# Six instead of seven chunks of the first MLP beside attention, and the fetch of a narrow input as a step of its own

## The chip, the cores and the metric

One core of one Trainium2 chip runs the kernel. The metric is the device time of one execution in microseconds; the figure for the kernel before is a median of 3 runs. Engines: PE is TensorE (PEld its weight loads), DVE VectorE, ACT ScalarE, POOL GpSimd, SP the engine whose queue issues the DMAs here.

## The reference

Attention over 4 batches, 8 heads, 576 positions and 64 dimensions, mixed with a read from a memory matrix, and then two MLPs in a row over the 2304 = 4 x 576 tokens, all in float32 accuracy:

```python
def _attn_ref(q, k, v, M_prev, z_prev, beta):        # q, k, v: (4, 8, 576, 64)
    scores = scale * np.matmul(q, k.transpose(0, 1, 3, 2))   # causal
    ...                                              # softmax, a @ v -> local
    mem_out = einsum(phi(q), M_prev) / (einsum(phi(q), z_prev) + 1e-06)
    g = 1.0 / (1.0 + np.exp(-beta))
    return g * mem_out + (1 - g) * local
x = attn_out.transpose(0, 2, 1, 3).reshape(2304, 512)
h = x @ w_in                                         # (512, 2048)
x = where(h > 0, h, exp(min(h, 0)) - 1) @ w_out      # first MLP
h = x @ w_in2
out = maximum(0.01 * h, h) @ w_out2                  # second MLP
```

The MLP weights come in as 64-bit floats, so the kernel fetches pairs of 32-bit words and decodes them.

## The kernel before

Products are made float32-accurate by splitting an operand into a high and a low part (xh, xl; gh, gl; two layers of w), three matmuls for one. The 2048 hidden units of an MLP are 16 chunks of 128. A chunk's weights (`load_w`, L92) are fetched raw, 1 MB in two DMAs, and decoded by ACT, DVE and POOL into the two layers; beside attention in halves through a PSUM bank, later whole, through one staging tile `wm` (one buffer from then on).

Attention runs batch by batch, 4 head pairs a batch. Each output of the product with v (`pv`, L498) goes to DRAM: for batch 0 into `xm`, for the others, where a head's rows carry two halves that still have to be added, into `xq`.

The first MLP is done in two ways. Its first `NFA` chunks are done **narrowly**, beside attention: each batch is cut into 2 parts of 288 tokens, 8 parts in all. `phase1_units` (L658) makes the list of steps of a batch's two parts. For each part: `u_x` fetches the input into the tile x (and, for batches 1 to 3, the other halves into y), adds the halves on DVE, splits the sum on ACT and POOL and writes the split parts to DRAM for later; then one `u_h` for each chunk, 12 matmuls of 288 columns into a `pm` bank, the activation (`elu`, ACT twice, DVE) and its split (ACT or DVE, POOL); then 4 `u_o`, 3 `NFA` matmuls each, whose result goes to DRAM. x and y have one buffer, xh and xl one for each of the two parts, gh and gl `NG` buffers, as many as there are chunks.

The other chunks are done **widely** after attention, in four tiles of 512 tokens and one of 256, with gh and gl in 3 buffers; narrow and wide results are added. The second MLP uses tiles of the same size and all 16 chunks.

What sets the order: the list of attention's steps has nominal costs of PE time. When the last step of a batch is listed, the steps of its narrow parts are appended to a list `fill`, due `DELAY` = 13000 ns of nominal cost later; from then on each attention step earns credit (`rate`, L749), and a fill step is put in when its cost is earned. `RESERVE` = 60000 ns of nominal cost is left for after attention, where `merge` (L706) mixes the remaining steps with the fetch and decode of the first `NPRE` = 6 of the wide chunks; the others follow in the first wide tile. The weights of the second MLP go into the slots of the narrow chunks during the later wide tiles and into those of the wide chunks after them. The order in this list is not the order on the engines. A planner at build time walks the whole program with estimated times and puts on each engine what is ready by then, earlier in the list first; a block under `high_priority(offset=FILL_OFF)` counts as 20 places earlier. What it lays down is fixed: on the chip an engine that comes to an instruction whose input has not landed stands there. The weights of the narrow chunks are in `wpa` and have a slot each; those of the wide chunks, in `wpb`, lie where attention's tiles were, so their fetch begins when attention has ended.

## Time and profile before

| | us |
|---|---|
| median of 3 runs | 1100.0 (1098.87 to 1101.18) |
| the profiled execution | 1098.26 |
| its span | 1096.2 |
| PE busy in the span | 1057.6 (96%) |
| DVE, ACT, POOL busy | 600.3, 484.8, 530.6 |
| granted TensorE clock, mean | 0.995 |

An engine's busy time is the sum of its instructions without overlap; PE's matmuls are pipelined, so the distance from one start to the next tells a matmul's cost better than its duration. A line such as L644 is a line of the kernel. "Idle before" in square brackets is the time an engine stood still ahead of an instruction, with what it was put down to. In the chain of waits each piece is a stretch of the work that ended last.

### The profile page before, as it was taken

What the parts mean: (1) busy time and instruction counts of PE and PEld (TensorE: products, weight loads), DVE (VectorE), ACT (ScalarE), POOL (GpSimd) and SP (SyncE); (2) the same over time, 40 slices, a digit from 0 to 9 for tenths busy, and PEclk for the clock granted to TensorE, in tenths of its full rate; (3) what the DMA queues carried; (4) which work ended last, traced back from release to release, by engine and by line L of the source; (5) the groups of instructions that cost most, each with busy time, mean ns of one, the idle gap of its engine ahead of it and who ended that gap; (6) DMA issues with size and microseconds to landing.
All of it is one profiled execution on the core that took longest, in us unless ns stands there. A gap on an engine that the chain in (4) does not pass through costs nothing.

```text
span 1096.2 us, 17406 instructions
## 1 busy us (share of the span) xinstructions
PE 1057.6 (96%) x5904; PEld 912.7 (83%) x5904; DVE 600.3 (55%) x1398; ACT 484.8 (44%) x1169; POOL 530.6 (48%) x674
## 2 busy tenths in 40 slices
PE   6998899989998999999999999999999999999997
PEld 3777789979998999978877889888888888888896
DVE  6889987778878857566574314664321222232232
ACT  5988877777877645444343223432211110111110
POOL 7675675667667626455453224755422322222221
PEclk9999999999999999999999999999999999999999
DMA  7753643564365139665653304331200100010010
GB/s 181 189 144 91 188 115 99 124 169 145 78 178 156 59 81 271 225 215 185 219 189 119 98 18 116 135 116 39 77 1 1 58 20 1 1 39 1 1 39 20
DMA packets 151576, 115.05 MB, mean 105 GB/s; under 512 B 81728, under 2 KB 144192, under 8 KB 151488
## 3 DMA queue, kind: packets, MB, share of 16 engines
q1 hardware_dynamic: 151488, 113.95, 35.5%
q8 instruction: 47, 0.77, 0.3%
q14 instruction: 41, 0.34, 0.1%
HBM read 78.52 MB, written 31.85 MB: 101 GB/s over the span
## 4 chain that ended last, share of the span: by engine, by line
PE 73%; DMA 8%; DVE 7%; POOL 3%; ACT 3%; SPq 3%; issue 3%; DVEq 0%; POOLq 0%; ACTq 0%
PE pm L616 17%; PE sc L876 14%; PE tp L616 13%; PE sc L644 8%; PE po L876 4%; PE pm L644 4%; PE po L522 3%; PE tp L455 3%; PE po L644 2%; DMA wraw<-in_moe_w_out_dram 2%; DMA x<-xq 2%; SPq L212 2%; PE sc L426 1%; PE sc L427 1%; PE pm L522 1%
## 5 line engine op out<-in xcount | busy, mean ns | idle before, releaser
L623 POOL TENSOR_TENSOR gl<-e,gh 128x512 fp32r<-128x512 f32 (+2 forms) x181 | 199.8, 1108 | 369.8 <-DVE gh L241 291.9
L616 PE MATMUL tp<-xw,w 128*128 128x512 f32 (+1 forms) x504 | 145.4, 371 | 0.9 <-DVE e L630 0.9
L616 PE MATMUL pm<-xw,w 128*128 128x512 f32 (+1 forms) x496 | 143.9, 371 | 0.0
L876 PE MATMUL sc<-w,gh 128*128 128x512 f32 x448 | 137.7, 393 | 0.0
L449 POOL TENSOR_SCALAR pt<-pt,rs,omg 128x128 f32<-128x128 f32 (+4 forms) x160 | 102.7, 651 | 28.0 <-DVE rs L444 25.7
L616 PEld LDWEIGHTS tp<-xw,w 128*128 128x128 f32 x504 | 91.3, 188 | 19.7 <-DVE e L630 1.7
L644 PE MATMUL sc<-gh,w 128*128 128x512 f32 (+2 forms) x438 | 106.0, 343 | 1.1 <-DVE st L857 0.7
L616 PEld LDWEIGHTS pm<-xw,w 128*128 128x128 f32 x496 | 90.5, 188 | 18.5
L434 ACT ACTIVATE pt<-pt,mx 128x128 f32<-128x128 f32 (+4 forms) x160 | 93.2, 585 | 22.7 <-DVE mx L429 22.1
L876 PEld LDWEIGHTS sc<-w,gh 128*128 128x128 f32 x448 | 83.1, 188 | 17.9
L616 PE MATMUL tp<-xv,w 128*128 128x512 f32 (+1 forms) x252 | 93.2, 370 | 0.0
L616 PE MATMUL pm<-xv,w 128*128 128x512 f32 (+1 forms) x248 | 92.0, 371 | 0.0
L616 PE MATMUL pm<-xh,w 128*128 128x288 f32 x368 | 80.2, 305 | 9.1 <-DVE e L630 5.7
L635 ACT ACTIVATE e<-pm 128x512 f32<-128x512 f32 (+1 forms) x40 | 22.2, 556 | 150.3 <-PE pm L616 149.1
L455 PE MATMUL tp<-ident,pt 128*128 128x128 f32 x480 | 80.1, 276 | 8.0 <-DVE al L248 3.1
L241 DVE CAST gh<-e 128x512 fp32r<-128x512 f32 (+2 forms) x146 | 77.9, 537 | 16.9 <-PE po L644 4.2
L137 POOL TENSOR_TENSOR w<-wm,w 128x512 fp32r<-128x512 f32 x50 | 66.1, 1344 | 43.4 <-ACT w L239 43.4
L876 PE MATMUL sc<-w,gl 128*128 128x512 f32 x224 | 85.4, 393 | 0.0
L644 PEld LDWEIGHTS sc<-gh,w 128*128 128x128 f32 x438 | 74.6, 188 | 12.2 <-issue 1.5
L636 DVE TENSOR_TENSOR e<-tp,e 128x512 f32<-128x512 f32 (+1 forms) x40 | 25.5, 637 | 107.2 <-ACT e L635 107.1
L636 DVE TENSOR_TENSOR e<-pm,e 128x512 f32<-128x512 f32 (+1 forms) x40 | 25.5, 637 | 105.8 <-ACT e L635 105.8
L429 DVE CUSTOM_DVE_ANT_0 pt<-sc,mask 128x128 f32<-128x128 f32 (+4 forms) x160 | 69.4, 446 | 8.6 <-PE sc L427 4.3
(155 smaller groups left out, 2407.9 us busy)
## 6 DMA issues: line engine op xcount, KB each, us to landing
wraw<-in_moe_w_in_dram SPq DMA_DIRECT2D x32, 512.0 KB, 4.1
wraw<-in_moe_w_out_dram SPq DMA_DIRECT2D x32, 512.0 KB, 5.3
xh<-xh SPq DMA_DIRECT2D x8, 576.0 KB, 3.3
xl<-xl SPq DMA_DIRECT2D x8, 576.0 KB, 3.9
ys<-st SPq DMA_DIRECT2D x32, 144.0 KB, 3.0
x1s<-st SPq DMA_DIRECT2D x36, 128.0 KB, 1.9
x<-x1s SPq DMA_DIRECT2D x9, 512.0 KB, 3.9
out_dram<-st SPq DMA_DIRECT2D x36, 128.0 KB, 1.7
```

The lines of the kernel that those rows point to most:

```text
L137: nc.gpsimd.tensor_tensor(out=w[:, 1, a], in0=t[:, a], in1=_f(w)[:, 0, a], op=ALU.subtract)
L241: (nc.vector if eng == "V" else nc.gpsimd).tensor_copy(dst, src)
L429: nc.vector.tensor_tensor_reduce(out=pt[0:m, k0:k0 + n], in0=sc[0:m, 0:n], in1=mk, op0=ALU.add, op1=ALU.min, scale=-0.125, scalar=mx[0:m, ...
L434: nc.scalar.activation(out=pt[0:m, 0:nk], in_=pt[0:m, 0:nk], func=AF.Exp, scale=-1.0, bias=mx[0:m, last:last + 1], accum_out=self.pd["ss"] ...
L449: nc.gpsimd.tensor_scalar(out=pt, in0=pt, scalar1=rs[0:m, i:i + 1], scalar2=omg[0:m, h:h + 1], op0=ALU.mult, op1=ALU.mult,)
L455: nc.tensor.transpose(dst, self.p[c][:, k0:k0 + kn], ident)
L522: nc.tensor.matmul(po[:, a:b], w, x, start=i == 0, stop=i == len(mms) - 1)
L616: nc.tensor.matmul(ph, wi[:, wj, kc, :], xx[:, kc, :], start=n_mm == 0, stop=n_mm == 11)
L623: nc.gpsimd.tensor_tensor(out=gl, in0=g, in1=_f(gh), op=ALU.subtract)
L636: nc.vector.tensor_tensor(out=t, in0=ph, in1=t, op=ALU.max)
L644: nc.tensor.matmul(py, wo[:, wj, ec * P:(ec + 1) * P], gg, start=opens and f == first and n_mm == 0, stop=closes and f == last and n_mm == 2,)
L876: nc.tensor.matmul(pos[tb], gg[:, tb * P:(tb + 1) * P], wo[:, wj, :], start=f == 0 and n_mm == 0, stop=f == NF - 1 and n_mm == 2,)
```

## The change

`NFA` and `NG` go from 7 to 6. `u_x` is cut into `u_load`, which issues the DMAs of a part's input, and `u_x`, which adds, splits and stores. Part 0's `u_load` is called as soon as its batch's last attention step is listed, ahead of the delay and outside the high priority; part 1's stands after the second `u_h` of part 0, and its `u_x` after the fifth `u_h` of part 0, ahead of the sixth and of the four `u_o`.

```diff
--- before.py
+++ after.py
@@ -44,7 +44,7 @@
     DFF = w1i.shape[1] // 2
     NKC = DM // P
     NF = DFF // P
-    NFA = 7
+    NFA = 6
     NPRE = 6
     NR = 3
     EB = 3
@@ -60,7 +60,7 @@
     TN = 256
     TW = 512
     NTT = NT // TN
-    NG = 7
+    NG = 6
     DSPAN = 0.75
     RESERVE = 60000.0
     EARLY = 150
@@ -657,32 +657,31 @@
 
     def phase1_units(ti):
 
-        units = []
-        for pi, (pt, o, w, _) in enumerate(parts):
-            if pt != ti:
-                continue
-            st = {}
-
-            def u_x(pi=pi, o=o, w=w, st=st):
-                def split():
-                    st["x"] = split_x(xt, w, pi % 2)
-                    for n in range(2):
-                        nc.sync.dma_start(xp_scr[n][pi], _f(st["x"][n]))
-                    st["g"] = {}
-
-                xt = mtile("x", 1, F32, (NKC, NW))[:, :, 0:w]
-                if ti < V32:
-                    nc.sync.dma_start(xt, xm_scr[ti][:, :, o:o + w])
-                    split()
-                    return
-                x2 = mtile("y", 1, F32, (NKC, NW))[:, :, 0:w]
-                for j in range(2):
-                    ps, pz = slice(64 * j, 64 * j + 64), slice(64 - 64 * j, 128 - 64 * j)
-                    nc.sync.dma_start(xt[ps], xq_scr[ti][j][ps, :, o:o + w])
-                    nc.sync.dma_start(x2[ps], xq_scr[ti][j][pz, :, o:o + w])
+        mine = [(pi, o, w, {}) for pi, (pt, o, w, _) in enumerate(parts) if pt == ti]
+
+        def u_load(pi, o, w, st):
+            xt = st["t"] = mtile("x", 1, F32, (NKC, NW))[:, :, 0:w]
+            if ti < V32:
+                nc.sync.dma_start(xt, xm_scr[ti][:, :, o:o + w])
+                return
+            x2 = st["t2"] = mtile("y", 1, F32, (NKC, NW))[:, :, 0:w]
+            for j in range(2):
+                ps, pz = slice(64 * j, 64 * j + 64), slice(64 - 64 * j, 128 - 64 * j)
+                nc.sync.dma_start(xt[ps], xq_scr[ti][j][ps, :, o:o + w])
+                nc.sync.dma_start(x2[ps], xq_scr[ti][j][pz, :, o:o + w])
+
+        def u_x(pi, o, w, st):
+            xt = st["t"]
+            if ti >= V32:
                 for c in range(NKC):
-                    nc.vector.tensor_tensor(out=xt[:, c], in0=xt[:, c], in1=x2[:, c], op=ALU.add)
-                split()
+                    nc.vector.tensor_tensor(out=xt[:, c], in0=xt[:, c], in1=st["t2"][:, c], op=ALU.add)
+            st["x"] = split_x(xt, w, pi % 2)
+            for n in range(2):
+                nc.sync.dma_start(xp_scr[n][pi], _f(st["x"][n]))
+            st["g"] = {}
+
+        units = [(0, lambda: u_x(*mine[0]))]
+        for k, (pi, o, w, st) in enumerate(mine):
 
             def u_h(f, w=w, st=st):
                 ph = h_bank()[:, 0:w]
@@ -696,12 +695,15 @@
                 copy(E_Y, y, py)
                 nc.sync.dma_start(y_scr[pi][:, ec], y)
 
-            units.append((0, u_x))
             for f in range(NFA):
                 units.append((HC * 12 * w / 2.4, lambda f=f, u=u_h: u(f)))
+                if k + 1 < len(mine) and f == 1:
+                    units.append((0, lambda k=k: u_load(*mine[k + 1])))
+                if k + 1 < len(mine) and f == NFA - 2:
+                    units.append((0, lambda k=k: u_x(*mine[k + 1])))
             for ec in range(NKC):
                 units.append((3 * NFA * w / 2.4, lambda ec=ec, u=u_o: u(ec)))
-        return units
+        return lambda: u_load(*mine[0]), units
 
     def merge(a, bu):
         ta = sum(c for c, _ in a) + 1.0
@@ -759,7 +761,9 @@
         if done == 0:
             close_decode()
         if done is not None:
-            fill += [(pos + DELAY, c2, u2) for c2, u2 in phase1_units(done)]
+            fetch, more = phase1_units(done)
+            fetch()
+            fill += [(pos + DELAY, c2, u2) for c2, u2 in more]
         if fill and fill[0][0] <= pos:
             credit += c * rate
         while fill and fill[0][0] <= pos and fill[0][1] <= credit:
```

## Rows read from the trace of the kernel before

**Rows 1.** Stages: us, busy (count) of PE, PEld, DVE, ACT, POOL, clock, DMA, GB/s.

```profile
0.00:104.00 104.00, 91.82 (x472) 69.52 (x473) 84.42 (x249) 84.94 (x234) 69.11 (x133) 1.00 0.59 153
104.00:211.00 107.00, 100.05 (x750) 94.97 (x750) 90.81 (x267) 83.46 (x241) 72.63 (x118) 1.00 0.47 128
211.00:313.00 102.00, 96.58 (x727) 94.07 (x726) 81.58 (x250) 77.85 (x221) 68.57 (x110) 0.98 0.53 137
313.00:404.00 91.00, 85.98 (x646) 83.65 (x645) 69.26 (x199) 61.31 (x171) 53.31 (x81) 0.98 0.40 112
```

**Rows 2.** Slices of 10 us beside attention, same columns.

```profile
130.00:140.00 10.00, 9.20 (x67) 8.43 (x66) 9.88 (x24) 8.52 (x27) 8.51 (x12) 1.00 0.76 220
...
240.00:250.00 10.00, 7.41 (x44) 7.08 (x45) 7.93 (x24) 7.38 (x22) 8.02 (x12) 0.83 0.63 178
```

**Rows 3.** Order of time on PE: stalls ahead of a narrow input's first matmuls.

```profile
121.37 0.81 PE L616 MATMUL pm<-xh,w 128*128 128x288 f32 x4 [1.85 <-ACT xh L239]
...
222.27 0.53 PE L616 MATMUL pm<-xh,w 128*128 128x288 f32 x2 [1.52 <-ACT xh L239]
...
244.50 0.53 PE L616 MATMUL pm<-xh,w 128*128 128x288 f32 x2 [2.59 <-DVE e L630]
...
338.16 0.85 PE L616 MATMUL pm<-xh,w 128*128 128x288 f32 x2 [2.83 <-DVE e L630]
```

**Rows 4.** Chain of waits: start us, us, a narrow and a wide run.

```profile
395.63 3.20 PE tp L616 x24
...
526.75 2.80 PE tp L616 x12
```

**Rows 5.** Order of time on PE: starts of two hidden chunks, last wide tile.

```profile
669.01 0.40 PE L616 MATMUL pm<-xw,w 128*128 128x256 f32 x2
...
670.41 0.40 PE L616 MATMUL tp<-xw,w 128*128 128x256 f32 x2
```

**Rows 6.** Order of time on SP: first weight fetch after attention.

```profile
408.18 0.53 SPq L102 DMA_DIRECT2D wraw<-in_moe_w_in_dram  x1
```

**Rows 7.** Order of time on POOL: ends of the wide chunks' decodes, nine in all.

```profile
422.94 2.62 POOL L137 TENSOR_TENSOR w<-wm,w 128x512 fp32r<-128x512 f32 x2
...
465.69 2.54 POOL L137 TENSOR_TENSOR w<-wm,w 128x512 fp32r<-128x512 f32 x2 [5.57 <-ACT w L239]
473.80 2.95 POOL L137 TENSOR_TENSOR w<-wm,w 128x512 fp32r<-128x512 f32 x2 [5.57 <-ACT w L239]
...
503.27 2.54 POOL L137 TENSOR_TENSOR w<-wm,w 128x512 fp32r<-128x512 f32 x2 [4.23 <-ACT w L239]
```

**Rows 8.** L644 (narrow outputs) by stage: us, busy (count) of PE, PEld, clock, DMA, GB/s.

```profile
104.00:211.00 107.00, 23.38 (x139) 19.69 (x140) 1.00 0.47 128
211.00:313.00 102.00, 27.30 (x164) 22.83 (x163) 0.98 0.53 137
313.00:404.00 91.00, 22.59 (x130) 18.62 (x130) 0.98 0.40 112
```

**Rows 9.** L616 (narrow hidden units) in the third of these stages, same columns.

```profile
313.00:404.00 91.00, 28.53 (x168) 24.68 (x168) 0.98 0.40 112
```

**Rows 10.** Order of time on POOL: decodes beside the second MLP's start, first and last.

```profile
681.20 2.60 POOL L137 TENSOR_TENSOR w<-wm,w 128x512 fp32r<-128x512 f32 x2
...
759.57 2.54 POOL L137 TENSOR_TENSOR w<-wm,w 128x512 fp32r<-128x512 f32 x2
```

**Rows 11.** Chain of waits: the second MLP's sixteenth chunk in its first tile.

```profile
768.60 2.80 PE tp L616 x12
```

**Rows 12.** Order of time on SP: batch 1's loads and the store before them.

```profile
192.79 0.54 SPq L681 DMA_DIRECT2D x<-xq  x1
...
211.03 0.41 SPq L530 DMA_DIRECT2D xq<-xp  x1
...
214.12 0.54 SPq L681 DMA_DIRECT2D x<-xq  x1
```

**Rows 13.** Order of time on DVE: the add on the same input.

```profile
221.29 2.17 DVE L684 TENSOR_TENSOR x<-x,y 128x288 f32<-128x288 f32 x4 [4.79 <-issue]
```

## The prediction

> **What bounds the kernel now.** I read the page's busy shares first, then the busy time by stage, then tens of microseconds inside the attention stage, then the order of time on SP, PE, DVE and POOL where PE falls short. TensorE is busy nearly everywhere: in the three stages in which attention and the first MLP's narrow parts run together, 104 to 404 us, it has 100.05, 96.58 and 85.98 us of 300, so it idles 17.4 us there [rows 1]. The reader is to see that DVE is never far behind (90.81 of the first 107 us), and that in a slice such as 130 to 140 it is DVE at 9.88 of 10 that sets the pace and PE that has room [rows 1, 2]. The kernel is therefore bound by PE's total work, plus some 17 us of stalls beside attention, plus what the weight decode lets through when attention ends.
>
> The stalls beside attention lie where a narrow part's input arrives. PE stood 1.85, 1.52, 2.59 and 2.83 us before the first matmuls on a new input (part 0 of batch 0, part 0 and part 1 of batch 1, part 1 of batch 2), 8.8 us in all [rows 3]. The one at 244.5 has a second cost: the granted clock of these ten microseconds is 0.83, a mean over 2.4 GHz and its half, so 1.7 us more are lost [rows 2].
>
> **Part 1: chunks moved from narrow to wide.** A chunk costs, in the narrow form, 24 matmuls in each of 8 parts, 192 of 288 columns. A run of 24 lasts 3.20 us, so one starts every 0.133 us, and the chunk is 192 x 0.133 = 25.6 us [rows 4]. In the wide form it is 24 matmuls in each of four tiles of 512 columns and one of 256. Twelve of the first take 2.80 us (0.233 each) [rows 4], and twelve of the second run from 669.01 to 670.41 (0.117 each) [rows 5]. So 96 x 0.233 + 24 x 0.117 = 25.2 us. The work on PE falls by 0.4 us: the move as such buys nothing, and the question is what it does to the waits.
>
> Beside attention, PE loses up to 25.6 us of work. Where PE is full this shortens the stage by as much. Where DVE is full, as in 130 to 140, it shortens nothing [rows 2]. One chunk's narrow part takes with it only eight DVE operations on the activation, a few microseconds. PE idles 17.4 of these 300 us, in slices in which it has room; an estimate: a quarter of the chunk's work falls into such slices, and a third of that is not returned, 2 us. Bounds: 0 (all slices full, as the 96.58 of 102 suggest) and +6 (a quarter of 25.6, none of it returned). I take +2.
>
> One weight chunk less is fetched and decoded beside batch 0, and one more after attention. PE is busy 91.82 of the first 104 us, and its idle time lies before 30 us, where loads land late [rows 1]; I take 0. Less traffic at the start could give 2 us, a different order of the first loads could take 2.
>
> **Part 2: the decode after attention.** This is the dear part. The chunks that are not done narrowly are decoded one after the other, in the space that attention leaves: one staging buffer, so ACT, DVE, DVE, DVE, ACT and two POOL operations are a chain. Its first fetch goes out at 408.18 [rows 6], and the two POOL operations that end each of nine chunks start at 422.94 to 503.27: eight steps, 10.0 us each, 8.1 us where nothing disturbs (465.69 to 473.80) [rows 7]. The first wide tile needs a chunk per 24 x 0.233 = 5.6 us of PE work. So the decode is slower than its user, and only work that PE has left over covers it.
>
> Before, this just fits. Of 3 x 168 narrow output matmuls of batches 0 to 2, 139 + 164 + 130 = 433 had run by 404 [rows 8], and the hidden ones of batch 2 all (168) [rows 9]. Left over are 71 and batch 3's 336: 407 x 0.133 = 54.3 us. With eight wide chunks of 5.6 us that is 99.1 us, to 503.1; the ninth chunk's first half is decoded at 503.27 + 1.3 = 504.6. Short by 1.5 us.
>
> After, there are ten chunks: the chain is one step longer, 8.1 to 10.0 us, I take 9: 100.6 + 9 = 109.6 us behind attention's end. The leftover shrinks with the chunk: 288 of batch 3 and 6/7 of 71, 349 x 0.133 = 46.5 us; nine wide chunks are 50.4; together 96.9. Short by 12.7 where it was 1.5: +11.2. Against that, with three buffers for activations PE can take up to two hidden chunks (2.8 us each) of the second wide tile early, 5.6 us. I take +5.6. Bounds: 0, if batch 2's leftover is so much larger that all of it is covered; +20, if batch 2 leaves nothing (288 x 0.133 = 38.4, so 88.8 against 110.6, less 1.5) and nothing is taken early. The reserve that the emission keeps for after attention is the same 60 us of nominal cost in both kernels, but the trace shows that the fill runs ahead of its place in the list, so fewer matmuls are likely to be left.
>
> In sentences of its own: the Trainium skill, page "TensorE: Matmul & The Clock Gate", section "HAM oscillation — how this bites in real kernels", says that a PE that waits between bursts of matmuls is put back to half its clock and pays for the return each time. The trace agrees where PE stood 2.59 us (0.83 in that slice). By that rule a starved first wide tile would cost up to 1.7 us more for each of its two or three gaps.
>
> The second MLP's weights go the same way: ten instead of nine chunks are decoded into the later slots, beside the last wide tile and the first of the second MLP. The last of nine starts its two POOL operations at 759.57, so its first half is there at 760.9 [rows 10], and PE takes it up at 768.60 [rows 11], 7.7 us later. A tenth comes one step later, (759.57 - 681.20) / 8 = 9.8 us, while the last wide tile, beside which the chain begins, is 24 x 0.117 = 2.8 us longer: 7.7 + 2.8 - 9.8 = 0.7 us of cover remain. I take 0, bounds 0 and +3.
>
> **Part 3: the fetch set apart.** The loads of a narrow part move ahead in the list: part 0's to where its batch ends, 13 us of nominal cost earlier; part 1's into the hidden chunks of part 0. The add and the split of part 1 move ahead of part 0's output. But a place in the list is only a priority: what is ready is issued. Batch 1's first load went out at 192.79, long before the list reaches it, and the one that needed the last store (issued 211.03) at 214.12 [rows 12]. The add on DVE could start only at 221.29 [rows 13]. Ahead of that add DVE stood idle 4.79 us, since the planner had taken the loads for landed. Neither the data nor the single buffer of x and y comes free earlier in the new list, so most of this wait stays. What can change is SP's order: part 1's load no longer stands behind key and value loads. I take -2. Bounds: -10.5 (all 8.8 us of PE's stalls and 1.7 us of clock), and +3.1, if the fetch of part 0 now stands at the head of SP's queue through the 3.1 us from store to load, with the next pair's loads and the copies of the keys' halves behind it and PE waiting for these.
>
> Sum against the profiled execution, 1098.3 us (span 1096.2 and 2.1 around it): -0.4 + 2 + 0 + 5.6 + 0 - 2 = +5.2, 1103.5. That execution lies 1.7 below the median of the runs shown, so **1105 us**.
>
> **Rivals.** *The fetch pays.* The adds no longer stand in DVE's queue ahead of their data, and the next part's split is done before it is wanted. For it: stalls at four inputs, and 4.79 us of idle DVE ahead of one add [rows 13]. Against it: the loads already go out as soon as they can [rows 12]. Then -10.5 takes the place of -2, and with DVE free the 2 us of part 1 go too: -0.4 + 5.6 - 10.5 = -5.3, 1095 on the scale of the median; if the decode is covered as well, 1089. It decides from the point where the fetch saves more than 7 us.
>
> *It cancels.* The order changes everywhere, and the decode step comes out at its undisturbed 8.1 us, because less narrow work competes with it on DVE and POOL: ten steps then take little more than nine did. For it: a mean step of 10.0 beside the 8.1 of an undisturbed one [rows 7]. Then +5.6 falls to about +1 and the sum to 0.6, 1101.
>
> *The first wide tile starves.* No leftover from batch 2 and nothing taken early: +20 instead of +5.6, 1098.3 + 19.6 + 1.7 = 1120. For it: fill runs ahead of its list, so with less of it batch 2 may be done when attention ends. Against it: PE and not DVE holds most of attention, so fill and attention shorten together.
>
> *SP is held.* In sentences of its own: the Trainium skill, page "DMA: Bandwidth & Descriptors", section "Anatomy of one DMA — SWDGE (gpsimd) path", says that a DMA's semaphore wait is served on the issuing sequencer, ahead of dispatch, so a load that waits holds what is queued behind it. The trace agrees: 3.1 us from the last store to the load that needs it. By rows, three batches at +3.1 instead of -2 give 1098.3 + 7.2 + 9.3 + 1.7 = 1116.5.
>
> **How the numbers follow.** The forecast (1101 to 1110) gets 0.38, the paying fetch 0.33, cancelling 0.18, the starved tile 0.06, the held queue 0.05. A measurement of this kernel tells about 0.2%, 2.2 us. Faster takes the paying fetch: 0.33. Within 2.2 us: most of the cancelling case and a little of the forecast, 0.18. Slower: 0.49. The range for 8 in 10 has cases of both signs in it: 1090 to 1114; the forecast's own is 1101 to 1110.
>
> **What would show it.** Right: narrow records fall by 192 and wide ones rise by 120; attention's last matmuls come some 15 us earlier; ten pairs of POOL decode operations follow, with PE gaps of microseconds before the last hidden chunks of the first wide tile; the adds on DVE still wait 2 to 5 us. Wrong: no PE gap between attention's end and the second wide tile, or no idle DVE ahead of the adds and a granted clock of 1.0 all through attention. Either of these alone takes away the term that makes the sum positive.

## The result, and the profile after

The changed kernel takes 1108.61 us (median of 6 runs, 1104.72 to 1111.48) where the kernel before takes 1098.61 in the same session: 1.0086 times, 95% interval 1.0068 to 1.0104. It is slower by 0.9%. The forecast was 1105 with a range of 1090 to 1114. The profiled execution of after took 1111.48 us (span 1109.4, granted clock 0.988), 2.9 above its median; differences below that are taken from profiled executions carry this.

First the page's busy times for the whole span, then the busy time by stage (columns as in [rows 1]; attention's last product with v starts at 387.77, the first wide matmul at 441.32).

```profile
PE 1066.9 (96%) x5832; PEld 915.5 (83%) x5832; DVE 589.3 (53%) x1392; ACT 483.0 (44%) x1156; POOL 532.7 (48%) x673
```

```profile
0.00:104.00 104.00, 93.28 (x477) 71.40 (x477) 80.42 (x239) 84.13 (x231) 69.42 (x134) 0.98 0.55 143
104.00:204.00 100.00, 95.94 (x709) 93.14 (x709) 83.47 (x257) 78.67 (x228) 68.14 (x112) 0.97 0.50 136
204.00:304.00 100.00, 93.67 (x697) 91.29 (x697) 81.72 (x249) 75.57 (x217) 66.07 (x107) 0.97 0.53 139
304.00:388.00 84.00, 76.07 (x543) 70.58 (x543) 65.05 (x199) 59.05 (x167) 51.39 (x81) 0.98 0.44 121
388.00:441.00 53.00, 49.82 (x357) 48.80 (x356) 31.61 (x52) 24.52 (x52) 28.24 (x30) 0.97 0.78 248
441.00:504.00 63.00, 61.11 (x275) 49.57 (x274) 38.74 (x41) 26.89 (x36) 31.78 (x24) 1.00 0.51 169
```

The matmul records are 5832 where they were 5904: 192 fewer narrow ones, 120 more wide ones. Attention ends 16.2 us earlier than before (404.0, the end of the last stage in [rows 1]), and the three stages from 104 to 388 us have 18.3 us of PE idle in 284, about as much as before in 300. But the granted clock, which was 1.00, 0.98, 0.98, is 0.97, 0.97, 0.98. Then 3.2 of 53 and 1.9 of 63 us are idle behind attention.

What fills attention: the narrow hidden units (L616) and narrow outputs (L644) by stage, columns us, busy (count) of PE, PEld, clock, DMA, GB/s; they answer to [rows 8, 9].

```profile
104.00:204.00 100.00, 26.27 (x144) 21.37 (x144) 0.97 0.50 136
204.00:304.00 100.00, 24.43 (x144) 20.91 (x144) 0.97 0.53 139
304.00:388.00 84.00, 20.21 (x120) 17.87 (x121) 0.98 0.44 121
```

```profile
104.00:204.00 100.00, 25.52 (x144) 20.70 (x144) 0.97 0.50 136
204.00:304.00 100.00, 24.08 (x144) 20.22 (x144) 0.97 0.53 139
304.00:388.00 84.00, 11.38 (x72) 9.90 (x72) 0.98 0.44 121
```

A batch has 144 of each now. In the first two stages all 144 hidden and all 144 outputs are done inside the stage: at the hand-over to the next batch nothing narrow is left to fill PE with. In order of time on PE no narrow matmul starts from 198.78 to 213.14 and from 299.65 to 310.99, nor for 21.5 us from 345.23 in batch 3. Before, 139 and 164 of 168 outputs were done there, so some stood over [rows 8], and the longest such stretch up to attention's end was 9.4 us, in batch 3. What that looks like: a slice of ten microseconds in the first of the two stretches, the gap in it in order of time on PE, and the adds it waits behind on VectorE (DVE); square brackets are the idle time ahead and its releaser.

```profile
210.00:220.00 10.00, 7.46 (x34) 7.29 (x35) 6.51 (x22) 4.26 (x12) 6.71 (x11) 0.66 0.65 157
```

```profile
212.54 0.58 PE L426 MATMUL sc<-kk,qs 128*128 128x256 f32 x1 [3.78 <-DVE mx L429]
```

```profile
210.91 1.20 DVE L677 TENSOR_TENSOR x<-x,y 128x288 f32<-128x288 f32 x3 [2.89 <-DMA y<-xq]
```

DVE stands 2.89 us at an add whose data has not landed; the scores' maxima behind it on DVE come late, and PE, with no narrow work to put in, stands 3.78 us. The slice's clock is 0.66, a mean over 2.4 and 1.2 GHz, and its 7.46 busy us hold only 34 matmuls.

Two more gaps of about 2 us or more stand beside attention. They do not lie where narrow work has run out: narrow matmuls start within 4 us ahead of each and 2 us after it. PE waits there for DVE, the second time for an operation behind the adds of the next part's input.

```profile
128.36 0.44 PE L337 MATMUL sc<-ident,qn 128*128 128x128 f32 x2 [1.98 <-DVE mx L429]
...
329.89 0.94 PE L455 MATMUL tp<-ident,pt 128*128 128x128 f32 x6 [2.33 <-DVE al L248]
```

```profile
326.90 2.53 DVE L677 TENSOR_TENSOR x<-x,y 128x288 f32<-128x288 f32 x4 [1.35 <-DMA kk<-kk]
329.35 0.88 DVE L248 TENSOR_TENSOR al<-tp,ah 128x320 fp32r<-128x320 f32 x2
```

Five slices between 100 and 388 us have a clock below 1. Weighted with PE's busy time in each, it costs 7.4 us there, against 2.7 us before.

Behind attention, the decode of the wide chunks' weights: the first fetch in order of time on SP, and the POOL operations that end the first and the tenth of ten chunks, beside [rows 6, 7].

```profile
392.81 0.54 SPq L102 DMA_DIRECT2D wraw<-in_moe_w_in_dram  x1
```

```profile
406.54 2.60 POOL L137 TENSOR_TENSOR w<-wm,w 128x512 fp32r<-128x512 f32 x2
...
496.68 2.55 POOL L137 TENSOR_TENSOR w<-wm,w 128x512 fp32r<-128x512 f32 x2 [4.23 <-ACT w L239]
```

From the fetch to the last pair it is 103.9 us, 95.1 before: +8.8, one step. But PE has no gap before the last hidden chunks of the first wide tile, from 470 to 520 us none. Its gaps are earlier, and they have another releaser: PE's two largest, then DVE ahead of each.

```profile
418.99 1.06 PE L644 MATMUL sc<-gh,w 128*128 128x288 f32 x6 [2.68 <-DVE gh L241]
...
458.17 0.73 PE L616 MATMUL tp<-xw,w 128*128 128x512 f32 x2 [1.89 <-DVE e L630]
```

```profile
412.99 2.18 DVE L677 TENSOR_TENSOR x<-x,y 128x288 f32<-128x288 f32 x4 [1.18 <-DMA wraw<-in_moe_w_in_dram]
415.09 1.30 DVE L127 TENSOR_SCALAR wm<-wm 128x1024 int32<-128x1024 int32 x1
...
416.67 1.44 DVE L128 SCALAR_TENSOR_TENSOR wm<-wraw,wm 128x1024 int32<-128x1024 int32 x1
418.04 0.89 DVE L241 CAST gh<-e 128x288 fp32r<-128x288 f32 x1
```

```profile
454.30 0.69 DVE L127 TENSOR_SCALAR wm<-wm 128x1024 int32<-128x1024 int32 x1 [4.98 <-ACT wm L126]
455.03 1.23 DVE L128 SCALAR_TENSOR_TENSOR wm<-wraw,wm 128x1024 int32<-128x1024 int32 x1
456.29 1.22 DVE L131 SCALAR_TENSOR_TENSOR wm<-wraw,wm 128x1024 int32<-128x1024 int32 x1
457.43 0.68 DVE L630 SCALAR_TENSOR_TENSOR e<-e,tp 128x512 f32<-128x512 f32 x1
```

At 458.17 PE waits for an activation (L630) that is queued on DVE behind the three operations of a decode, 3.1 us. At 418.99 it waits for a cast (L241) that stands behind the last input's adds, 2.18 us, and two operations of a decode, 1.30 and 1.44 us. So in this kernel the decode reaches PE through DVE's queue, not through weights that come late; at the larger gap the adds stand in that queue too.

### The profile page after: what moved, and what is told of

Same layout as the page of the kernel before. It is cut to its first block, busy times and chain, and to the rows that moved or that the text cites. A ratio compares the mean times of both kernels' runs of the same rounds, so it can differ in the third digit from the quotient of the medians.

```text
span 1109.4 us, 17233 instructions
## 1 busy us (share of the span) xinstructions
PE 1066.9 (96%) x5832; PEld 915.5 (83%) x5832; DVE 589.3 (53%) x1392; ACT 483.0 (44%) x1156; POOL 532.7 (48%) x673
## 4 chain that ended last, share of the span: by engine, by line
PE 71%; DVE 9%; DMA 7%; POOL 4%; ACT 4%; issue 3%; SPq 2%; DVEq 0%; ACTq 0%; POOLq 0%
PE pm L616 16%; PE sc L880 14%; PE tp L616 12%; PE sc L644 7%; PE po L880 4%; PE pm L644 3%; PE po L522 3%; PE tp L455 3%; PE pm L522 2%; POOL w L137 2%; DMA wraw<-in_moe_w_in_dram 1%; PE po L644 1%; DVE wm L128 1%; PE sc L426 1%; PE sc L427 1%
## 5 line engine op out<-in xcount | busy, mean ns | idle before, releaser
L616 PE MATMUL tp<-xw,w 128*128 128x512 f32 (+1 forms) x520 | 150.8, 371 | 1.9 <-DVE e L630 1.9
L616 PE MATMUL pm<-xw,w 128*128 128x512 f32 (+1 forms) x520 | 150.6, 371 | 0.2 <-DVE e L630 0.2
L644 PE MATMUL sc<-gh,w 128*128 128x512 f32 (+2 forms) x492 | 121.0, 345 | 5.0 <-DVE gh L241 2.7
L616 PEld LDWEIGHTS tp<-xw,w 128*128 128x128 f32 x520 | 94.4, 188 | 21.4 <-DVE e L630 2.3
L616 PEld LDWEIGHTS pm<-xw,w 128*128 128x128 f32 x520 | 94.5, 188 | 19.7 <-DVE e L630 0.7
L434 ACT ACTIVATE pt<-pt,mx 128x128 f32<-128x128 f32 (+4 forms) x160 | 93.1, 584 | 18.4 <-DVE mx L429 14.2
L644 PEld LDWEIGHTS sc<-gh,w 128*128 128x128 f32 x492 | 84.1, 189 | 18.1 <-issue 3.8
L616 PE MATMUL pm<-xv,w 128*128 128x512 f32 (+1 forms) x260 | 96.4, 371 | 0.0
L616 PE MATMUL tp<-xv,w 128*128 128x512 f32 (+1 forms) x260 | 96.4, 371 | 0.0
L635 ACT ACTIVATE e<-tp 128x512 f32<-128x512 f32 (+1 forms) x40 | 22.2, 554 | 144.6 <-PE tp L616 144.6
L241 DVE CAST gh<-e 128x512 fp32r<-128x512 f32 (+2 forms) x148 | 72.2, 491 | 17.2 <-PE po L644 4.0
L644 PE MATMUL sc<-gl,w 128*128 128x512 f32 (+2 forms) x246 | 77.3, 345 | 0.2 <-POOL gl L623 0.2
L429 DVE CUSTOM_DVE_ANT_0 pt<-sc,mask 128x128 f32<-128x128 f32 (+4 forms) x160 | 69.4, 447 | 10.5 <-PE sc L427 4.7
```

What stands on the lines that cost most here:

```text
L241: (nc.vector if eng == "V" else nc.gpsimd).tensor_copy(dst, src)
L429: nc.vector.tensor_tensor_reduce(out=pt[0:m, k0:k0 + n], in0=sc[0:m, 0:n], in1=mk, op0=ALU.add, op1=ALU.min, scale=-0.125, scalar=mx[0:m, ...
L434: nc.scalar.activation(out=pt[0:m, 0:nk], in_=pt[0:m, 0:nk], func=AF.Exp, scale=-1.0, bias=mx[0:m, last:last + 1], accum_out=self.pd["ss"] ...
L616: nc.tensor.matmul(ph, wi[:, wj, kc, :], xx[:, kc, :], start=n_mm == 0, stop=n_mm == 11)
L644: nc.tensor.matmul(py, wo[:, wj, ec * P:(ec + 1) * P], gg, start=opens and f == first and n_mm == 0, stop=closes and f == last and n_mm == 2,)
```

## How the runs are read: two terms

For each run two numbers are taken from its profiled execution. **Term A** is what attention didn't give back: the narrow work taken out of attention, less the microseconds by which it ends earlier than 404.0. **Term B** is what the rest (span less attention's end, 692.2 us before) is longer than its work: less 25.2 us for each chunk done widely more, and less the narrow matmuls left over beyond 410 (their number before), each 0.133 us [rows 4, 5]. "Left" counts the matmuls of 288 columns that start after attention's last product with v. The work taken out is 25.6 us for each chunk less, plus 0.133 us for each matmul more left over. A + B - 0.4 for each chunk moved is the difference of the spans.

```
kernel                            chunks  left  taken out  earlier     A      B   ratio to before [95%]
before                                 7   410        0.0      0.0   0.0    0.0
after                                  6   384       22.1     16.2   5.9    7.7   1.0086 [1.0068, 1.0104]
e1 fetch apart, seven                  7   399       -1.5     -5.6   4.1    0.7   1.0032 [1.0013, 1.0051]
e2 six, fetch as before                6   384       22.1     14.0   8.1    6.1   1.0098 [1.0071, 1.0126]
e3 held, six                           6   409       25.5     20.8   4.7    5.8   1.0092 [1.0074, 1.0110]
e4 held, seven                         7   415        0.7      4.1  -3.4    0.1   0.9991 [0.9977, 1.0004]
e5 six, 7th's weights early            6   359       18.8     10.6   8.2    1.7   1.0068 [1.0039, 1.0097]
e6 five                                5   414       51.7     30.8  20.9   25.7   1.0409 [1.0376, 1.0441]
e9 six, reserve 37                     6   288        9.4      9.4   0.0   14.4   1.0131 [1.0105, 1.0158]
e10 six, reserve 83                    6   605       51.5     32.0  19.5   10.2   1.0288 [1.0259, 1.0318]
e11 seven, reserve 83                  7   599       25.1      7.8  17.3    2.1   1.0146 [1.0116, 1.0176]
e12 held, seven, reserve 50            7   336       -9.8     -9.1  -0.7   12.2   1.0111 [1.0082, 1.0139]
e13 held, six, 7th's weights early     6   414       26.1     24.2   1.9    1.7   1.0009 [0.9986, 1.0033]
e14 held, seven, reserve 70            7   518       14.4     10.4   4.0   -1.3   1.0004 [0.9987, 1.0022]
```

The two terms come from one execution of each kernel, and executions differ: those of after lie between 1104.72 and 1111.48 us, and the profiled one lies between 3.6 us below the median of its kernel (e4) and 2.9 us above it (after, e11). A difference of A or B of a few microseconds between two runs is therefore a hint; the ratio is made from all executions.

## The experiments

**e1 and e2: each part of the change alone.** The first is the changed kernel with seven chunks, the second the kernel before with six:

```diff
-    NFA = 6
+    NFA = 7
-    NG = 6
+    NG = 7
```

```diff
-    NFA = 7
+    NFA = 6
-    NG = 7
+    NG = 6
```

> Seven chunks as before, with the fetch set apart. If the six chunks make the change slower and the fetch does little, as forecast: ratio to before 0.997 to 1.002, DVE still idle 2 to 5 us ahead of the adds of batches 1 to 3, granted clock about 0.995. If it is the fetch that costs (its loads ahead in SP's queue, the add of part 1 ahead of part 0's output): 1.005 to 1.009. If the fetch pays: below 0.996.

> Six chunks with the fetch as before. If the six chunks are the cost: 1.006 to 1.011, with nearly all of batch 0's and 1's narrow matmuls done inside their stages, PE idle of 2 us and more where a batch's input arrives, and a granted clock near 0.988. If the fetch is the cost: 0.998 to 1.002.

Six chunks alone cost 1.0098, the fetch alone 1.0032; both together 1.0086. The slowdown is that of six chunks. The fetch set apart wins nothing: it costs 0.3% with seven chunks, and with six it makes no difference that the intervals separate. DVE's idle time ahead of the first of the four adds on each input beside attention (batches 1 and 2, order of time on DVE) is 12.1 us in all before, 8.3 in e1, 4.5 in e2 and 4.7 in after: it falls with the chunk, and of these four the two in which it is smallest are the slower ones.

**e3 and e4: the adds held.** The adds of batches 1 to 3 are put on DVE behind the last listed copy of attention's output, so that DVE no longer stands at them beside attention, and the narrow steps fall due earlier. e3 is this on the changed kernel, e4 the same with `NFA = NG = 7`.

```diff
-    DELAY = 13000.0
+    DELAY = 5000.0
...
-            nc.vector.tensor_copy(xp, po[:, 0:n])
+            behind[0] = nc.vector.tensor_copy(xp, po[:, 0:n])
...
-                for c in range(NKC):
-                    nc.vector.tensor_tensor(out=xt[:, c], in0=xt[:, c], in1=st["t2"][:, c], op=ALU.add)
+                with tc.issue_after(behind[0].ins):
+                    for c in range(NKC):
+                        nc.vector.tensor_tensor(out=xt[:, c], in0=xt[:, c], in1=st["t2"][:, c], op=ALU.add)
```

> The changed kernel with the adds of batches 1 to 3 queued on DVE behind the last attention output copy listed ahead of them, and a delay of 5000 instead of 13000. If the stalls where an input arrives come from DVE standing at the add ahead of its data: DVE idle ahead of the adds below 1 us each, PE idle there below 1 us, clock back to 0.994 or more, ratio to before 0.999 to 1.004. If they come from the lack of narrow work to cover the hand-over: PE idle stays at 2 to 4 us at each arrival, ratio 1.007 to 1.011.

> The same hold with seven chunks. If DVE standing at the add is what the arrivals cost, the 10.5 us of stalls and clock that the kernel before shows there go for the most part: ratio 0.990 to 0.996. If the arrivals cost nothing that a hold can give back: 0.998 to 1.003.

With seven chunks it wins back the 0.3% of e1 and a little more (0.9991, not told apart from before). With six it wins nothing in the time (1.0092), though DVE's idle time ahead of those adds is gone: A is 4.7 where it was 5.9, B 5.8 where it was 7.7. So DVE standing at the adds is not what six chunks cost, or only its smaller part. What a good attention looks like is in e4, its stages in the columns of [rows 1]: as much idle as elsewhere, but a full clock all through, in every slice.

```profile
100.00:200.00 100.00, 93.68 (x713) 90.40 (x712) 83.14 (x248) 79.25 (x228) 69.77 (x113) 1.00 0.46 127
200.00:300.00 100.00, 93.94 (x703) 89.42 (x702) 84.09 (x247) 75.07 (x215) 67.92 (x107) 1.00 0.54 141
300.00:400.00 100.00, 95.38 (x716) 91.43 (x715) 79.10 (x229) 69.63 (x198) 59.76 (x93) 1.00 0.41 115
```

This execution is the fastest of e4's twelve (1094.70; their median is 1098.32). In it, too, no narrow matmul starts for 14.8 us from 207.4 and for 25.5 us from 315.1, and yet PE never stands longer than 1.4 us beside attention. So a stretch without narrow work does not by itself make the gap of 3.78 us that after has; the adds that DVE stands at are part of it.

**e5: is B the tenth decode?** Six chunks are done narrowly, but the weights of the seventh are decoded beside batch 0 as before, so nine are left for the chain after attention.

```diff
+    NWA = 7
...
-    dec = [lambda f=f: load_w(0, wpa, w1i, w1o, f, f) for f in range(NFA)]
+    dec = [lambda f=f: load_w(0, wpa, w1i, w1o, f, f) for f in range(NWA)]
...
-    wun = [(1, lambda f=f: load_w(0, wpb, w1i, w1o, f, f - NFA)) for f in range(NFA, NF)]
+    wun = [(1, lambda f=f: load_w(0, wpb, w1i, w1o, f, f - NWA)) for f in range(NWA, NF)]
```

(The two lists of the second MLP's weights and the spacing of the decodes beside batch 0 change in the same way.)

> The changed kernel with six chunks done beside attention, but the weights of the seventh chunk are decoded beside batch 0 as before the change, and its chunk is then done wide; so nine pairs, not ten, are left for the chain of decodes after attention. Theory (the time after attention that six chunks add is the tenth step of that chain): the first-half decode that ends last comes some 9 us earlier against the first fetch after attention (96 us, not 105), TensorE's gaps between attention's end and the second MLP fall from 7.5 to 3 to 4 us, and the ratio to before is 1.003 to 1.005 instead of 1.0086; what is left lies in attention, whose end stays at 386 to 389 us. Rival (the chain costs nothing, all of the loss lies in attention and in the granted clock): ratio 1.007 to 1.010.

Order of time on SP and on POOL: the first fetch after attention, and the ninth and last pair of the first MLP:

```profile
397.60 0.54 SPq L103 DMA_DIRECT2D wraw<-in_moe_w_in_dram  x1
```

```profile
492.04 2.55 POOL L138 TENSOR_TENSOR w<-wm,w 128x512 fp32r<-128x512 f32 x2 [4.23 <-ACT w L240]
```

The chain is 94.4 us long, as before (95.1), and B falls from 7.7 to 1.7. That half of the theory stands in the trace. The ratio, 1.0068, is above what the theory gave, and its interval reaches to both expectations and to the 1.0086 of after; A is 8.2, since attention ended at 393.4, not at 386 to 389. That early weights win time is clear of the noise only in e13.

**e6: five chunks.** `NFA = NG = 5` in the changed kernel.

> The changed kernel with five chunks instead of six beside attention (eleven done wide). Theory (each chunk taken from attention leaves 6 to 8 us of its 22 us unreturned there, and adds a decode step of 9 to 10 us to the chain after it, of which 5 to 7 us show): attention ends at 370 to 373 us, ratio to before 1.018 to 1.024. Rival 1 (attention is bound by its own chain of waits with six already, so that nothing more is returned): it ends at 383 to 388 us, ratio 1.027 or more. Rival 2 (attention gives back all of the chunk's work, and the seventh chunk's loss was in a single place): it ends at 364 to 366 us, ratio 1.009 to 1.014.

1.0409, far above the theory's 1.024, though attention ends at 373.2, about where the theory had it (the rival with so large a ratio had it at 383 to 388). A is 20.9 of 51.7 us, and B has a new member: ahead of the first narrow matmuls after attention PE stands 15.89 us (order of time on PE), and two slices are nearly empty.

```profile
396.62 0.85 PE L616 MATMUL pm<-xh,w 128*128 128x288 f32 x2 [15.89 <-ACT xh L239]
```

```profile
380.00:390.00 10.00, 0.72 (x6) 0.49 (x4) 5.08 (x7) 3.32 (x7) 3.31 (x4) 0.73 1.06 316
390.00:400.00 10.00, 3.38 (x14) 3.38 (x15) 4.55 (x7) 3.76 (x6) 5.84 (x6) 0.50 0.95 313
```

180 hidden matmuls are left after attention: the last batch's 120 and the 60 of part 1 of batch 2. The list says why. With this little credit no step of batch 2 has been written into the order when batch 3 is handed over (its part 0 runs early all the same, by its priority); the changed kernel then issues batch 3's first fetch at once, and it takes the one tile x ahead of part 1 of batch 2. That part is fetched only at 386.34, after batch 3's add at 381.27, but its matmuls stand first in PE's queue. So e6 measures, beside the chunk, a fetch that goes out too early, and is no measure of a chunk's price.

**e9 and e10: more and less filling.** Only `RESERVE` changes in the changed kernel, to 37000 and to 83000.

```diff
-    RESERVE = 60000.0
+    RESERVE = 37000.0
```

> The changed kernel with RESERVE 37000 instead of 60000, which brings the planner's rate of filling back to that of before (0.86 instead of 0.66 us of narrow work for each us of attention): some 23 us of narrow work move from after attention into it. Theory A (attention's loss is that its filling runs out at each hand-over): attention ends at 402 to 406 us, PE stalls at the hand-overs and the slices of low clock go, and 5 to 7 us are won there; but only some 17 us of narrow work cover the decodes after attention, so TensorE waits for the chain 5 to 15 us more there: ratio 1.008 to 1.018. Theory B (attention is bound by something that filling doesn't change, the fall-off of the returned work is a fixed loss): ends at 410 us or later, ratio above 1.018. Rival C (cover after attention is plentiful): ratio 1.002 to 1.005.

> The changed kernel with RESERVE 83000: some 23 us of narrow work move out of attention to after it, where they cover the chain of ten decodes. Theory A (filling is what attention lacks): attention ends only 12 to 16 us earlier, at 372 to 376 us, with more gaps of TensorE and a lower clock in it; after it the cover grows and TensorE's gaps there fall from 7.5 to 3 to 4 us: ratio 1.009 to 1.014. Rival (attention returns what is taken from it, the decode chain is what costs): attention ends at 365 to 367 us and the ratio is 1.002 to 1.005.

With 37000, 13 us more than in after run beside attention, not the 23 expected, and attention ends 6.8 us later, at 394.6 and not at 402 to 406 (A falls from 5.9 to 0.0): the other half fell into time that PE lost anyway. The ratio lies in theory A's range, but by another way: B rises to 14.4, and not by the decodes, as was expected. Attention's last product is at 394.60; of the hidden matmuls the last batch's 144 are left, and no others; and that batch's input takes 10.5 us through store, load, add and split, in which PE has nothing else (order of time on PE):

```profile
405.12 0.85 PE L616 MATMUL tp<-xh,w 128*128 128x288 f32 x2 [10.12 <-ACT xh L239]
```

With 83000 some 29 us less lie beside attention, of which 15.8 come back; it ended at 372.0, as theory A had it, but the ratio 1.0288 is far above its 1.014, and B did not fall. More was moved than the expected 23 us, and this run too has the fetch in the wrong order. SP's loads of inputs and DVE's adds:

```profile
284.08 0.54 SPq L670 DMA_DIRECT2D x<-xq  x1
...
291.48 0.55 SPq L670 DMA_DIRECT2D x<-xq  x1
...
304.57 2.15 SPq L670 DMA_DIRECT2D x<-xq  x2
```

```profile
297.62 2.38 DVE L677 TENSOR_TENSOR x<-x,y 128x288 f32<-128x288 f32 x3
...
312.39 3.01 DVE L677 TENSOR_TENSOR x<-x,y 128x288 f32<-128x288 f32 x4
```

The first two loads wait for batch 2's stores, and what comes behind them, at 304.57, is part 1 of batch 1, a whole batch late. Its hidden units cannot fill the stage that they were listed for:

```profile
200.00:250.00 50.00, 12.05 (x72) 10.45 (x72) 0.97 0.49 129
250.00:300.00 50.00, 0.00 (x0) 0.00 (x0) 0.96 0.53 130
300.00:350.00 50.00, 9.05 (x48) 7.62 (x48) 0.90 0.46 133
```

(These are the narrow hidden units, L616, by 50 us.) That the order is turned round is read from these rows and from how many steps the list still held at the hand-overs; no run here undoes that alone.

**e11: the same, with seven chunks.** The kernel before with `RESERVE = 83000.0`: filling is taken away, and chunks, decodes and matmuls stay.

> The kernel before (seven chunks, fetch and adds together) with RESERVE 83000 instead of 60000: as much narrow work is moved out of attention as with the six-chunk run at 83000, and the number of chunks, of decodes and of matmuls is that of before. Theory (narrow work taken out of attention comes back only in part, about 55%, whatever takes it out, since attention is then held by its own chain and by a clock that falls with TensorE's gaps): some 23 to 29 us leave it, attention ends 12 to 17 us earlier (387 to 392), and the ratio is 1.008 to 1.014. Rival (what costs is the number of chunks: the wide tiles and the tenth decode): attention returns all of it, ratio 0.998 to 1.003.

1.0146, nearly all of it in A: 25.1 us taken out, 7.8 given back; B is 2.1. Here the fetch is in the old place, so no input is out of order: filling taken out of attention brings an A with no chunk less, and the rival, that attention returns all of it, is refuted. The theory had the cause with too small a price (31% came back, not 55%). From 350 to 380 us PE starts only 21 narrow matmuls; two slices of these 30 us, with all engines:

```profile
350.00:360.00 10.00, 7.22 (x41) 6.74 (x42) 9.42 (x26) 5.60 (x16) 8.20 (x12) 0.83 0.54 163
360.00:370.00 10.00, 7.98 (x52) 6.34 (x52) 9.50 (x34) 8.27 (x24) 6.14 (x11) 1.00 0.21 80
```

PE is busy 7.22 and 7.98 where DVE is at 9.42 and 9.50: here attention by itself goes at DVE's pace, and PE had room for narrow matmuls beside it.

**e12 and e14: is there something better with seven?** The kernel of e4 with `RESERVE` 50000 and 70000.

> Seven chunks, with the fetch apart and the adds held behind the listed copy of attention's output (as in e4_held_seven), and RESERVE 50000 instead of 60000: some 10 us of narrow work more beside attention. Theory (half of what is put into attention is hidden there, and what it lacks as cover after attention turns up as waits for the decodes or for the last batch's input): attention ends 5 to 7 us later than in e4 (405 to 407), TensorE's gaps after it rise from 3.5 to 6 to 10 us, ratio to before 0.997 to 1.003. Rival (cover after attention is still plentiful with nine decodes): gaps stay at 3 to 4 us, ratio 0.994 to 0.997.

> As e4_held_seven (seven chunks, adds held), with RESERVE 70000: some 10 us of narrow work less beside attention. Theory (about half of it comes back): attention ends 4 to 7 us earlier than in e4 (393 to 396), the gaps after it stay at 3 to 4 us, ratio 1.002 to 1.006. Rival (with the adds held attention gives back all of it): it ends at 390 us, ratio 0.997 to 1.000.

No. At 50000 attention ends at 413.1, and PE stands 8.53 us for the last batch's input; 1.0111. The expectation, 0.997 to 1.003, missed: here the filling costs nearly its full price in attention (9.1 of 9.8 us), and the cover for the last batch's input is gone at once. At 70000 attention keeps 4.0 us in the profiled execution, of which a smaller B gives back 1.3; that execution is 1.6 us above its kernel's median. By the medians the time is that of before: 1.0004, below the 1.002 to 1.006 expected, though attention ended at 393.6, where the theory had it.

**e13: both cures on six chunks.** The edits of e3 and e5 together.

> Six chunks narrow with the seventh's weights kept beside batch 0 (as in e5_seventh_kept), and the adds held (as in the held kernels). Theory (three parts that add up: the tenth decode is gone, the add no longer stands on VectorE, and attention gives back only part of the chunk): ratio 1.002 to 1.006. Rival (the hold gains nothing with six chunks, as e3_held_six had it beside e2_six_only): ratio 1.006 to 1.009, that of e5.

1.0009 [0.9986, 1.0033]: six chunks cost no measurable time any more. A is 1.9 and B 1.7; of 26.1 us taken out, 24.2 come back. It is better than the theory's 1.002 to 1.006, though the interval reaches into that range. Early weights beside held adds win 0.8% (1.0092 to 1.0009), without them 0.2% with overlapping intervals (1.0086 to 1.0068). Why the two help each other, with A the lower by 6.3 from e5 to e13, no run here tells apart. The clock does not explain it: in five slices up to attention's end it is below 1 in e13 too, which costs 5.8 us, though PE never stands longer than 1.4 us there. One of them:

```profile
220.00:230.00 10.00, 8.47 (x50) 6.79 (x48) 9.62 (x28) 8.62 (x23) 4.52 (x9) 0.83 0.44 110
```

PE is at 8.47 of 10 in it and DVE at 9.62.

No version beats the kernel before; e4, e13 and e14 are level with it.

## Why the prediction was right, and where not

The side, the range and the case (the forecast's own slope, not a rival) were right. The terms:

**PE's work, -0.4.** Right: the records changed by -192 and +120.

**Attention not returning PE work, +2 with bounds 0 to +6.** This is the term that was mis-sized: 5.9 in after, 8.1 in e2, at and above the upper bound. Two things were missing in it. The share: the estimate took a quarter of the chunk's work to lie in slices where PE has room, a third of that not returned. In after 27% is not returned (5.9 of 22.1), and in e11, with seven chunks, 69%. And the clock: PE's idle time in attention hardly changed (18.4 us before, 19.1 after from 100 us on), but the largest gap now falls where nothing narrow is left, and the slices at a lower clock cost 7.4 instead of 2.7 us. That is most of A in the profiled execution of after, but not in every run: the same sum is 4.3 and 4.1 us in e2 and e5, whose A is 8.1 and 8.2, and 5.8 in e13, whose A is 1.9. So the size of A is measured, and its make-up is not settled. The prediction had named the first hint, a slice at 0.83 [rows 2], but used it for the fetch alone, and it did not read the second one, 0.91 and 0.92 from 330 to 350.

In sentences of its own: the Trainium skill, page "TensorE: Matmul & The Clock Gate", section "HAM oscillation — how this bites in real kernels", says that a matmul kernel whose bursts are shorter than the waits between them starts each burst at half clock. The runs agree in direction (0.66 in the slice with the 3.78 us gap, 0.73 and 0.50 in the two with the 15.89 us gap), though PE, busy for 96% of the span in after, has bursts there that are longer than its waits; e4, with no such slice beside attention, is the fastest profiled execution (span 1092.9).

**The amount taken out.** The prediction let the leftover shrink from 407 to 349 matmuls. It went from 410 to 384. The reserve for after attention is 60 us of nominal cost in both kernels, so a chunk less is taken nearly wholly out of attention: 22.1 us where 17.9 were expected. The prediction had named this reserve and then argued it away by the fill running ahead of its place. Hence attention's end 16.2 us earlier, near the 15 forecast, is a larger cut with a larger loss in it.

**The decode beside batch 0, 0 with bounds of 2 either way.** Right in size. With a decode less, PE is busy for 93.28 us of the first 104, where it was 91.82 [rows 1], but the granted clock there is 0.98 and not 1.00, which takes about as much. e5 and e13, which put the decode back, have A higher by 2.3 and lower by 2.8 than after and e3, so they show no side.

**The decode after attention, +5.6.** Right in size: B is 7.7, 6.1 and 5.8 with ten decodes (after, e2, e3), and 1.7 twice with nine (e5, e13), so the tenth step is worth 4.1 to 6.0 in these single executions. By the medians it is worth 0.2% without held adds, not clear of the noise, and 0.8% with them. The chain did grow by 8.8 us where 9 were forecast. The place was wrong: no gap stood before the last hidden chunks. The larger leftover covers the weights, and what PE waits for in after is activations behind decode operations on DVE. In e2 PE idles 5.0 us from attention's end to 560 (6.4 in after), and 3.0 of them are put down to the split of the last input, on ACT and POOL. So that the tenth decode costs is shown; by which wait it does is read from one trace.

**The second MLP's decode, 0.** Right: from 700 us to the end of the span PE idles 5.8 us in both kernels (396.2 less 390.4, 409.4 less 403.6).

**The fetch set apart, -2.** No gain: +3.5 us with seven chunks (0.32% in e1), and no difference that can be measured with six. The prediction had the adds still waiting 2 to 5 us, with the data no earlier. In after one of four inputs beside attention is like that (2.89 us); DVE waits 1.35 us at most at the others. This came with the chunk (4.5 us in all in e2), not with the fetch (8.3 in e1). With seven chunks attention lost 4.1 us in the execution of e1, a little more than the bound of +3.1. The 3.1 us from store to load behind that bound were also not a queue held still: SP issued five other loads in them before the change.

```profile
211.54 2.03 SPq L212 DMA_DIRECT2D qn<-in_q_dram  x4
213.66 0.41 SPq L227 DMA_DIRECT2D zb<-in_z_prev_dram  x1
```

What was not seen at all is that an early fetch through one tile x can overtake the part before it (e6, e10); in after it does not, since there the list has put in part 1's fetch by each hand-over.

**The sum.** +5.2 was forecast against +13.2 between the profiled executions and +10.0 between the medians. The difference of 8.0 is A (3.9 more than forecast), the decode (2.1 more) and the fetch (2 that did not come), so the forecast fell short on the same side in three terms. Of its signs, the records, the ten pairs and attention's end came true; the gaps before the last hidden chunks and the adds that wait 2 to 5 us did not, but for one add. The rivals: the paying fetch (0.33) is refuted by e1 and e2. The cancelling case would have needed ten steps in the time of nine. The starved tile and the held queue gave too much; but a starved PE after attention does occur where less is left over, by the last batch's input and not by the decodes (e9, e12).

What stays open: of the 13.2 us between the profiled executions, clock and idle time account for 11.1 (4.7 and 0.7 from 100 us to attention's end, 1.7 and 4.0 from there to 560 us), by slices of ten microseconds. The clock of one kernel's executions moves by some thousandths from run to run, so the split is that of one execution. That the lower clock follows from the gaps was seen side by side in the slices of after, and no run changed the one without the other; in e13 the clock fell without a gap of that size.

## What to carry to other kernels

Work that is laid beside another stage is worth less or more than its own time there: measure the exchange by moving only the amount (here the reserve), before the form of the work is changed. When a reserve is a fixed amount, a cut of the total comes nearly wholly out of the other side. And where a chain of decodes and the activations share an engine, a step more of the chain can show up in that engine's queue, and not where the chain ends.

## What the runs showed that was not expected

The amount beside attention has a steep side. Putting 10 us more in costs 1.2% over e4 (e12), while taking 14 out costs nothing that can be measured (e14) and taking 25 out, without the held adds, costs 1.5% (e11). The steep side is there because the last batch's narrow work can only start some 10 us after attention's last product (394.60 to 405.12 in e9) and needs other work in front of it. And a mean clock hides what a few slices cost: in after it is 0.988, but from 100 to 560 us the loss stands in six slices of ten microseconds, five of which hold or follow a gap of PE of only 2.0 to 3.8 us (at 128.36, 212.54, 329.89 and 418.99).
